# Replacing a scheduled work list by one that every engine follows literally, in an attention and mixer kernel on one core

## The chip, the cores and the metric

The kernel runs on one NeuronCore of a Trainium2 chip. The metric is the device time of one execution in microseconds; the number of record is the median of the timed runs. The core has five engines that are used here: TensorE (PE, with its weight loads shown as PEld), VectorE (DVE), ScalarE (ACT), GpSimd (POOL) and SyncE (SP), which only starts DMAs. Each engine works through its own queue of instructions in order and waits on semaphores.

## The reference

Inputs are q, k and v of shape (8 batches, 8 heads, 576 positions, 64), and four weight matrices. All are float32, and so is the output of shape (8, 576, 512).

```python
def _attn_ref(q, k, v):
    scores = scale * np.matmul(q, k.transpose(0, 1, 3, 2))
    rel = pos[:, None] - pos[None, :]
    mask_plain = (rel >= 0) & (rel < window)                                # 32; heads 0 to 3
    mask_dil = (rel >= 0) & (rel < window * dilation) & (rel % dilation == 0)  # 32*4; heads 4 to 7
    scores = np.where(masks, scores, -1e9)
    attn = softmax(scores)
    return attn @ v
def _moe_ref(x, w_tok1, w_tok2, w_ch1, w_ch2):       # x: (8, 576, 512), heads side by side
    xt = x.transpose(0, 2, 1)
    h = np.maximum(xt @ w_tok1, 0.0) @ w_tok2        # mixes positions, 576 -> 256 -> 576
    u = x + h.transpose(0, 2, 1)
    h2 = np.maximum(u @ w_ch1, 0.0) @ w_ch2          # mixes channels, 512 -> 1536 -> 512
    return u + h2
```

## The kernel before

The kernel handles the eight batches one after the other in a software pipeline: while PE does the channel mixing of batch n, the attention and the token mixing of batch a = n + 1 are worked in between.

**Loads.** `load_qk` brings q or k of four heads (a "kind": 0 for the plain window, 1 for the dilated one) into one buffer `lqk` with five DMAs; there are four such buffers, filled in the order q0, k0, q1, k1. `load_v` brings v with five larger DMAs into `lv`. All of these are started by SP, as are the copies inside the chip: `shift_v` (2 DMAs), `perm_v` (8 DMAs, rows of v in the dilated order), `x_perm` and `x_perm4` (4 DMAs each, attention results back to the natural order, for positions 0 to 511 and 512 to 575), and the output DMAs in `y_out`. The weights are loaded by POOL's queue in `wload`, which converts them to 16 bits on the way.

**Attention.** The loaded pieces are converted to 16 bits (`cast_qk`, `cast_v`; on POOL, for batch 0 on DVE), transposed on PE with the copy out on ACT (`tr`), and multiplied in small blocks (`qk_run`, three units u = 0, 1, 2, each with two halves). Each half goes through `sm_max` (DVE: mask add and row maximum), `sm_sub` (POOL: subtract), `sm_exp` (ACT), `sm_tr` (DVE: transposes of 32x32 blocks). `av_run` multiplies with v in three PSUM banks per kind and `av_out` (DVE) divides by the row sums.

**Mixing.** `h1_` and `u_` are the two matmuls of the token mixing; the last two matmuls of each `h1_` read the rows that `x_perm4` brings. `ut_` transposes the result. `m1_` (matmuls named gp, results gt) and `y_mm` (matmuls named yp) are the channel mixing, 12 blocks and 5 row tiles per batch; `y_out` adds u and starts the output DMA.

**Order.** Each of these steps is put in a list with `at(t, fn, ...)`, where t is a hand-written time, and the list is emitted sorted by t. In the kernel before, that order is only a priority: a planner in the compiler, which has its own cost model, picks for each engine the next instruction that it holds to be ready. So the order in each engine's queue can differ from the list. `gate` writes one element of `w1` from `lqk[("q", 1)]`, so that the load of `w1` comes after q1 has landed; nothing holds back the other weights.

Of the kernel before, what the change touches and what calls it, by code (L numbers as in the profile page):

```python
# [15 lines left out]
B = 8  # L16
H = 8
S = 576
# [4 lines left out]
NEG = -1.0e30  # L23

# [5 lines left out]
def _np_masks():  # L30
    q = np.arange(32)[:, None]
    j = np.arange(64)[None, :]
    base = np.where((j > q) & (j <= q + 32), 0.0, NEG).astype(np.float32)
    first = base.copy()
    first[:, 0:32] = NEG
    m8 = np.zeros((4, 32, 2, 2, 4, 64), dtype=np.float32)
    for g in range(4):
        for s in range(4):
            m8[g, :, 0, :, s] = (first if (s == 0 and g == 0) else base)[:, None]
            m8[g, :, 1, :, s] = (first if s == 0 else base)[:, None]  # L40
    m4 = np.broadcast_to(base[None], (4, 32, 64))
    return (np.ascontiguousarray(m8.reshape(128, 2, 8, 64)),
            np.ascontiguousarray(m4.reshape(128, 1, 64)))
# [3 lines left out]
def kernel(  # L47
# [15 lines left out]
    items = []  # L63

# [4 lines left out]
    m8_np, m4_np = _np_masks()  # L69
    ident = sb.tile([128, 128], FP16, tag="ident", name="ident")  # L70
    mask8 = sb.tile([128, 2, 8, 64], FP32, tag="mask8", name="mask8")
    mask4 = sb.tile([128, 1, 64], FP32, tag="mask4", name="mask4")
# [4 lines left out]
    qT = [one([128, 4, QTW], FP16, f"qT{i}") for i in range(2)]  # L77
    kT = [one([128, 4, KTW], FP16, f"kT{i}") for i in range(2)]
# [14 lines left out]
    def init():  # L93
        nc.scalar.dma_start(out=ident, in_=nc.inline_tensor(np.eye(128, dtype=np.float16), name="ident128").ap())
        nc.scalar.dma_start(out=mask8, in_=nc.inline_tensor(m8_np, name="mask8_d").ap())
        nc.scalar.dma_start(out=mask4, in_=nc.inline_tensor(m4_np, name="mask4_d").ap())
        for i in range(2):
            e = nc.vector
            e.memset(qT[i][:, :, S:QTW], 0.0)
            e.memset(kT[i][:, :, 0:KTO], 0.0)  # L100
            e.memset(kT[i][:, :, KTO + S:KTW], 0.0)
# [8 lines left out]
        nc.vector.memset(w1b[0:64], 0.0)  # L110

# [40 lines left out]
    def tr(n, nm, kind, hh, eng):  # L152
        src = cq[(nm, kind)]
        hp = 2 * kind + hh
        p = ps.tile([128, 1024], FP16, tag="tp", bufs=2, name=f"tp_{nm}_{n}_{hp}")
# [6 lines left out]
        dst, o = (qT[n % 2], 0) if nm == "q" else (kT[n % 2], KTO)  # L162
# [8 lines left out]
    def qk_mm(n, sc, cell, kind, hh, s):  # L171
        par, hp = hh % 2, 2 * kind + hh // 2
        r0 = 64 * par
        for g in range(4):
            if kind == 0:
                t0 = 128 * s + 32 * g
                lhs = qT[n % 2][r0:r0 + 64, hp, t0:t0 + 32]
                rhs = kT[n % 2][r0:r0 + 64, hp, KTO + t0 - 32:KTO + t0 + 32]
            else:
                t0 = 128 * s + g  # L180
                lhs = qT[n % 2][r0:r0 + 64, hp, t0:t0 + 125:4]
                rhs = kT[n % 2][r0:r0 + 64, hp, KTO + t0 - 128:KTO + t0 + 125:4]
            yield dict(out=sc[32 * g:32 * g + 32, cell, :], lhsT=lhs, rhs=rhs, start=True, stop=True)
# [32 lines left out]
    def sm_max(n, u, par):  # L216
# [4 lines left out]
        if u < 2:  # L221
            nc.vector.tensor_tensor(out=s32, in0=sc, in1=mask8[:, u], op=ALU.add)  # L222
        else:
            a0, a1 = bass.broadcast_tensor_aps(sc[:, 0:4], mask4)
# [27 lines left out]
    BANKS = [(14, 20), (0, 7), (7, 14)]  # L252

    def av_run(n, kind):
        V_own = (vp if kind == 0 else vd)[n % 2]
        V_prv = (vs if kind == 0 else vd)[n % 2]
        for bi, (c0, c1) in enumerate(BANKS):
            av = ps.tile([128, 7, 65], FP32, tag="at", bufs=3, name=f"av_{n}_{kind}_{bi}")
            for c in range(c0, c1):
                s, hh = c // 4, c % 4  # L260
                par, kk = hh % 2, hh // 2
                if s < 4:
                    aT, cell = AT[(n, kind, par)], 4 * kk + s
                else:
                    aT, cell = AT[(n, 2, par)], 2 * kind + kk
                for half in (1, 0):
                    for g in range(4):
                        skip_prev = s == 0 and (kind == 1 or g == 0)
                        if half == 0 and skip_prev:
                            continue  # L270
                        rows = slice(32 * g, 32 * g + 32)
                        if half == 1:
                            rhs = V_own[rows, s, hh, :]
                        elif kind == 0:
                            rhs = V_prv[rows, s, hh, :]
                        else:
                            rhs = V_prv[rows, s - 1, hh, :]
                        nc.tensor.matmul(  # L278
                            out=av[rows, c - c0, :], lhsT=aT[rows, cell, half, :], rhs=rhs,
                            start=(half == 1), stop=(half == 0 or skip_prev),  # L280
                            tile_position=(32 * g, 32 * g),
                        )
            AV[(n, kind, bi)] = av
# [26 lines left out]
    H1, U, UT, GT, YP = {}, {}, {}, {}, {}  # L310
    MX = 3

    def mxp(name):
        return ps.tile([128, 512], FP32, tag="mx", bufs=MX, name=name)

    def h1_(n, jb):
# [9 lines left out]
        nc.tensor.matmul(out=p[:, 256:512], lhsT=w1b[:, js], rhs=x4, start=False, stop=True)  # L326
        t = sb.tile([128, DM], FP16, tag="h1", bufs=4, name=f"h1_{n}_{jb}")
# [3 lines left out]
    def u_(n, s):  # L331
        p = mxp(f"up_{n}_{s}")
        x = X[n]
        if s < 4:
            for jb in range(2):
                nc.tensor.matmul(out=p, lhsT=w2[:, jb, 128 * s:128 * s + 128], rhs=H1[(n, jb)],  # L336
                                 start=(jb == 0), stop=(jb == 1))
            t = sb.tile([128, DM], FP16, tag="u16", bufs=8, name=f"u16_{n}_{s}")
            nc.vector.tensor_tensor(  # L339
                out=t.rearrange("p (a c) -> p a c", a=2), in0=p.rearrange("p (a c) -> p a c", a=2),  # L340
                in1=x[:, :, 4 * s:4 * s + 4, :].rearrange("p a h d -> p a (h d)"), op=ALU.add)
        else:
            for jb in range(2):
                for a in range(2):
                    nc.tensor.matmul(out=p[64 * a:64 * a + 64, 0:256], lhsT=w2[:, jb, 512:576],
                                     rhs=H1[(n, jb)][:, 256 * a:256 * a + 256],
                                     start=(jb == 0), stop=(jb == 1))
            t = sb.tile([128, 256], FP16, tag="u16_4", bufs=2, name=f"u16_{n}_4")
# [4 lines left out]
    def ut_(n, s, eng):  # L353
# [4 lines left out]
        nb = 4 if s < 4 else 2  # L358
        for cb in range(nb):
            nc.tensor.transpose(out=p[:, 128 * cb:128 * cb + 128], in_=t[:, 128 * cb:128 * cb + 128],  # L360
                                identity=ident)
        if s < 4:
# [10 lines left out]
    def m1_(n, mb):  # L373
        t = sb.tile([128, S], FP16, tag="gt", bufs=14, name=f"gt_{n}_{mb}")
        for sh in range(2):
            p = mxp(f"gp_{n}_{mb}_{sh}")
            for cb in range(4):
                nc.tensor.matmul(out=p[:, 0:288], lhsT=w3[:, cb, 128 * mb:128 * mb + 128],  # L378
                                 rhs=UT[n][:, cb, 288 * sh:288 * sh + 288],
                                 start=(cb == 0), stop=(cb == 3))  # L380
            dst = t[:, 288 * sh:288 * sh + 288]
            if sh == 0 or mb % 3 == 2:
                nc.scalar.activation(out=dst, in_=p[:, 0:288], func=AF.Relu)  # L383
            else:
                nc.vector.tensor_scalar_max(out=dst, in0=p[:, 0:288], scalar1=0.0)  # L385
        GT[(n, mb)] = t

    def y_mm(n, s, m0, m1):
# [12 lines left out]
        if m1 == 12:  # L401
            y_out(n, s)
# [14 lines left out]
    def wload(i):  # L417
        g = nc.gpsimd
        if i == 0:
            g.dma_start(out=w1, in_=moe_w_tok1[0:512, :].rearrange("(s p) j -> p s j", p=128))  # L420
            g.dma_start(out=w1a[0:64], in_=moe_w_tok1[512:576, :])
            g.dma_start(out=w1b[64:128], in_=moe_w_tok1[512:576, :])
            g.dma_start(out=w2, in_=moe_w_tok2.rearrange("(j p) t -> p j t", p=128))
        elif i < 5:
            c = 384 * (i - 1)
            g.dma_start(out=w3[:, :, c:c + 384],
                        in_=moe_w_ch1[:, c:c + 384].rearrange("(c p) m -> p c m", p=128))
        else:
            m = 3 * (i - 5)
            g.dma_start(out=w4[:, m:m + 3],  # L430
                        in_=moe_w_ch2[128 * m:128 * m + 384, :].rearrange("(m p) c -> p m c", p=128))

    def gate(src):
        nc.gpsimd.tensor_copy(out=w1[0:1, 0, 0:1], in_=src)


    P = 36.0
    TM = 60.0

    def tm(n):  # L440
        return TM + n * P

    KEYS = [("q", 0), ("k", 0), ("q", 1), ("k", 1)]

    def softmax(n, u, t):
        at(t, qk_run, n, u)
        for par in range(2):
            o = 1.5 * par
            at(t + 0.6 + o, sm_max, n, u, par)
            at(t + 2.0 + o, sm_sub, n, u, par)  # L450
            at(t + 3.2 + o, sm_exp, n, u, par)
            at(t + 4.4 + o, sm_tr, n, u, par)

    def attention(n, tcast, ttr, dtr, tqk, tavd, tavp, engs, tload=None):
        for i, (nm, hq) in enumerate(KEYS):
            at(tcast + 1.4 * i, cast_qk, n, nm, hq, engs[i % len(engs)])
# [108 lines left out]
```

## Time and profile before

| | |
|---|---|
| Median of 3 runs | 416.58 us (413.0 to 416.91) |
| Profiled execution | 419.19 us, span 417.4 us |
| PE busy | 322.4 us (77%) |
| DVE, ACT, POOL busy | 205.6, 130.6, 103.9 us |
| Mean granted PE clock | 0.95 |
| First gp matmul of batch 0 | 73.0 us after the start |

Times inside the profile count from the start of the span. A row of a timeline gives start, length, engine, line and operation; rows of the same kind that follow each other are merged, with their count behind x. SPq is SP's queue at work on starting a DMA. In groups the numbers behind the bar are busy time in us, mean ns of one, and the idle time before, with what ended it.

### The profile page before, as it was taken

The numbers are of one execution on the slowest core, as the hardware profiler recorded it, in microseconds if no ns is written. First come the engines' busy times: TensorE is split into PE (matmuls) and PEld (weight loads), VectorE is DVE, ScalarE is ACT, GpSimd is POOL, SyncE is SP. The second block draws the span as 40 slices with busy tenths as digits, with TensorE's granted clock in tenths as the row PEclk, the third lists the DMA queues.
The fourth block names the chain that finished last, engine by engine and source line by source line (L and its number), as shares of the span: only waits on it lengthen the run. The fifth ranks groups of instructions, "written<-read, shape, count | busy, mean of one in ns | idle before, by whom it ended". The sixth has DMA issues, their size and how long they took to land.

```text
span 417.4 us, 12992 instructions
## 1 busy us (share of the span) xinstructions
PE 322.4 (77%) x5680; PEld 204.4 (49%) x5680; DVE 205.6 (49%) x435; ACT 130.6 (31%) x273; POOL 103.9 (25%) x107
## 2 busy tenths in 40 slices
PE   0113148999399969869489989878998899799995
PEld 0012033854158536545336655655565556564763
DVE  4015743383344944863416743873277518764322
ACT  1113102740038305440513515341445133521420
POOL 7001322273106503530611224322333001300000
PEclk9999997999599989998869999998999899999999
DMA  9999246967365866395765567661310111012102
GB/s 186 192 207 219 63 106 151 196 161 167 94 136 149 173 162 171 87 210 149 157 146 152 129 135 202 163 128 37 130 39 2 33 51 59 9 31 78 38 27 88
DMA packets 131240, 50.24 MB, mean 120 GB/s; under 512 B 117360, under 2 KB 123888, under 8 KB 131184
## 3 DMA queue, kind: packets, MB, share of 16 engines
q1 hardware_dynamic: 126080, 45.06, 46.3%
q0 software_dynamic: 4672, 3.77, 5.6%
q8 instruction: 44, 0.72, 0.8%
q10 hardware_dynamic: 432, 0.59, 0.4%
q14 instruction: 12, 0.10, 0.1%
HBM read 36.44 MB, written 9.44 MB: 110 GB/s over the span
## 4 chain that ended last, share of the span: by engine, by line
PE 52%; SPq 18%; DVE 13%; issue 6%; DMA 3%; POOL 3%; ACT 3%; POOLq 0%; DVEq 0%
PE yp L394 20%; PE gp L378 12%; SPq L118 11%; PE av L278 5%; DVE mx L226 3%; PE h1p L321 3%; POOL s L232 3%; PE up L336 3%; DVE s L222 3%; SPq L126 2%; PE tpu L360 2%; ACT e L237 2%; PE tp_k L157 2%; DMA lk<-in_k_dram 2%; PE tp_q L157 2%
## 5 line engine op out<-in xcount | busy, mean ns | idle before, releaser
L378 PE MATMUL gp<-uT,w 128*128 128x288 f16 x768 | 108.7, 291 | 13.9 <-ACT gt L383 7.6
L378 PEld LDWEIGHTS <-w 128*128 128x128 f16 x768 | 73.3, 99 | 40.4 <-issue 21.0
L394 PE MATMUL yp<-w,gt 128*128 128x512 f16 x384 | 91.4, 391 | 2.2 <-issue 1.9
L232 POOL TENSOR_TENSOR s<-s,mx 128x512 f32<-128x512 f32 (+1 forms) x48 | 42.8, 899 | 102.4 <-DVE mx L226 93.6
L383 ACT ACTIVATE gt<-gp 128x288 f16<-128x288 f32 x128 | 50.4, 408 | 46.1 <-PE gp L378 42.0
L394 PEld LDWEIGHTS <-gt 128*128 128x128 f16 x384 | 37.4, 100 | 46.1 <-issue 8.0
L408 DVE TENSOR_TENSOR o<-yp,u 128x512 f32<-128x512 f32 x32 | 22.0, 689 | 67.4 <-PE yp L394 65.7
L385 DVE TENSOR_SCALAR gt<-gp 128x288 f16<-128x288 f32 x64 | 28.5, 449 | 29.0 <-PE gp L378 28.4
L164 ACT COPY qT<-tp_q 128x576 f16<-128x576 f16 x32 | 19.3, 643 | 71.0 <-PE tp_q L157 71.0
L237 ACT ACTIVATE e<-s 128x512 f16<-128x512 f32 (+1 forms) x48 | 26.7, 559 | 45.0 <-POOL s L232 45.0
L278 PEld LDWEIGHTS <-aT 32*32 32x32 f16 x2400 | 24.9, 94 | 30.4 <-issue 19.4
L245 DVE STREAM_TRANSPOSE aT<-e 128x512 f16<-128x512 f16 (+1 forms) x48 | 29.5, 618 | 17.0 <-ACT e L237 16.9
L133 POOL CAST cq<-lq 128x1280 f16<-128x1280 f32 x14 | 17.5, 1252 | 74.2 <-PE tp_q L157 42.7
L321 PE MATMUL h1p<-x,w 128*128 128x512 f16 x64 | 21.6, 472 | 13.3 <-DMA x<-xd 13.3
L164 ACT COPY kT<-tp_k 128x576 f16<-128x576 f16 x32 | 19.9, 641 | 28.5 <-PE tp_k L157 28.5
L226 DVE TENSOR_REDUCE mx<-s 128x8 f32<-128x512 f32 (+1 forms) x48 | 27.5, 577 | 0.2
L157 PE MATMUL tp_q<-ident,cq 128*128 128x128 f16 x160 | 13.4, 230 | 17.8 <-DVE cq L133 17.6
L328 ACT ACTIVATE h<-h1p 128x512 f16<-128x512 f32 x16 | 9.4, 597 | 56.4 <-PE h1p L326 56.4
L157 PE MATMUL tp_k<-ident,ck 128*128 128x128 f16 x160 | 14.4, 230 | 14.9 <-DVE ck L133 14.3
L222 DVE TENSOR_TENSOR s<-sc,mask 128x512 f32<-128x512 f32 x32 | 21.0, 676 | 9.5 <-PE sc L190 9.3
L339 DVE TENSOR_TENSOR u<-up,x 128x512 f16<-128x512 f32 x32 | 21.0, 686 | 9.3 <-PE up L336 8.9
L278 PE MATMUL av<-vd,aT 32*32 32x65 f16 x1152 | 14.2, 197 | 13.9 <-DMA vd<-vn 11.1
(58 smaller groups left out, 300.1 us busy)
## 6 DMA issues: line engine op xcount, KB each, us to landing
lq<-in_q_dram SPq DMA_DIRECT2D x64, 128.0 KB, 3.8
lk<-in_k_dram SPq DMA_DIRECT2D x64, 128.0 KB, 3.4
lv<-in_v_dram SPq DMA_DIRECT2D x32, 256.0 KB, 4.0
out_dram<-o SPq DMA_DIRECT2D x32, 256.0 KB, 2.3
w<-in_moe_w_ch_dram POOLq DMA_DIRECT2D x8, 384.0 KB, 15.8
vd<-vn SPq DMA_DIRECT2D x32, 65.0 KB, 2.1
x<-xd SPq DMA_DIRECT2D x32, 64.0 KB, 2.1
vs<-vp SPq DMA_DIRECT2D x8, 243.8 KB, 2.9
```

The costliest lines, as they stand in the source:

```text
L118: nc.sync.dma_start(out=t[0:np_, s], in_=src[n, 4 * kind:4 * kind + 4, 128 * s:128 * s + np_, :].rearrange("h p d -> p h d"),)
L157: nc.tensor.transpose(out=p[:, 128 * s:128 * s + 128], in_=src[:, s, 2 * hh:2 * hh + 2].rearrange("p a d -> p (a d)"), identity=ident,)
L164: nc.scalar.copy(out=dst[:, hp, o:o + S], in_=p[:, 0:S])
L222: nc.vector.tensor_tensor(out=s32, in0=sc, in1=mask8[:, u], op=ALU.add)
L226: nc.vector.tensor_reduce(out=mx[:, 0:nc_, 0], in_=s32[:, 0:nc_], op=ALU.max, axis=AX.X)
L232: nc.gpsimd.tensor_tensor(out=s32[:, 0:nc_], in0=a0, in1=a1, op=ALU.subtract)
L237: nc.scalar.activation(out=e16[:, 0:nc_], in_=s32[:, 0:nc_], func=AF.Exp, scale=0.125)
L278: nc.tensor.matmul(out=av[rows, c - c0, :], lhsT=aT[rows, cell, half, :], rhs=rhs, start=(half == 1), stop=(half == 0 or skip_prev), tile_ ...
L321: nc.tensor.matmul(out=p, lhsT=w1[:, s, js], rhs=x[:, :, 4 * s:4 * s + 4, :].rearrange("p a h d -> p a (h d)"), start=(s == 0), stop=False)
L378: nc.tensor.matmul(out=p[:, 0:288], lhsT=w3[:, cb, 128 * mb:128 * mb + 128], rhs=UT[n][:, cb, 288 * sh:288 * sh + 288], start=(cb == 0), s ...
L383: nc.scalar.activation(out=dst, in_=p[:, 0:288], func=AF.Relu)
L394: nc.tensor.matmul(out=p, lhsT=GT[(n, mb)][:, 128 * s:128 * s + 128], rhs=w4[:, mb], start=(mb == 0), stop=(mb == 11))
```

## The change

Five things change together.

1. **Literal order.** The list is emitted inside `tc.manual_schedule()`. Every engine, SP and POOL included, then issues its instructions exactly in the order of the list.
2. **A new list.** Its times are no longer fixed offsets in a period of 36 us. `place` walks a hand-written row of PE pieces (tokens: m and y for channel mixing, h, u, x for token mixing and its transposes, T for the transposes of q and k, Q for the scores, D and A for the value products of the dilated and plain heads) and adds up durations from the table `DUR`; each piece's follow-up on another engine is placed a little behind it. `need` moves a piece behind the time at which its inputs are expected. Matmuls and their evacuation, which were one function, are now two entries (`m1_mm`/`m1_out`, and so on), as are `tr_mm`/`tr_out`.
3. **Value products bank by bank.** `av_run` handles one PSUM bank per call, and other matmuls stand between the banks.
4. **Weights held back.** Every weight DMA on POOL now has its own one-element `gate`: the token weights and the first quarter of `w3` wait for k1 of batch 0, the rest of `w3` waits for v of batch 0, `w4` waits for k1 of batch 1; and the first load of batch 1 waits for the last quarter of `w3`.
5. **Small things.** The transposed q and k (`qT`, `kT`) have one buffer instead of two. The mask of 512 KB is built on chip from one of 96 KB. The banks are counted from the front.

The core of the diff:

```diff
+    BANKS = [(0, 7), (7, 14), (14, 20)]
+    def av_run(n, kind, bi):
...
+    def wload_ch1(i, after):
+        c = 384 * i
+        gate(w3[0:1, 0, c:c + 1], after)
+        nc.gpsimd.dma_start(out=w3[:, :, c:c + 384], ...)
...
+        elif kind in "DA":
+            _, a, bi = tok
+            kd = int(kind == "D")
+            t = need(t, ("s", a, kd), ("s", a, 2), ("v", a, kd))
+            at(t, av_run, a, kd, bi)
+            at(t + d + LAT, av_out, a, kd, bi)
+            ready(("x", a), t + d + LAT + 0.9)
+            if bi == 2:
+                at(t + d + LAT + 1.2, x_perm if kd else x_perm4, a)
+                ready(("x", a), t + d + LAT + 1.2 + 2.2)
...
+    def casts(a, ts, eng, load=True):
+        for i in range(4):
+            at(ts[i], cast_qk, a, *KEYS[i], eng[i % len(eng)])
+            ready(("c", a, i), ts[i] + 1.3)
+            if load:
+                loads_after(ts[i] + 1.3, a, i)
+        at(ts[4], cast_v, a, 0, eng[-1])
+        at(ts[4] + 1.3, shift_v, a)
+        at(ts[5], cast_v, a, 1, eng[-1])
+        at(ts[5] + 1.3, perm_v, a)
...
+        if load:
+            loads_after(ts[5] + 1.4, a, 4)
...
+    casts(0, [4.0, 7.0, 10.0, 13.5, 20.0, 21.0], [nc.vector], load=False)
...
+    t = run(-1, 24.5, [("D", 0, 0), ("D", 0, 1), ("D", 0, 2), ("A", 0, 2), ("A", 0, 0), ("A", 0, 1)])
...
+        if n == 0:
+            at(28.0, lambda: nc.gpsimd.tensor_copy(out=lqk[("q", 0)][0:1, 0, 0, 0:1], in_=w3[0:1, 0, 384 * 3:384 * 3 + 1]))
+            for i in range(4):
+                at(28.1, load_qk, 1, *KEYS[i])
+            at(28.2, load_v, 1)
+            for i in range(4):
+                at(30.0 + 0.1 * i, wload_ch2, i, lqk[("k", 1)][0:1, 0, 0, 0:1])
...
+        else:
+            toks = (M(0, 1) + [("Q", a, 1)] + M(2, 3, 4) + [("Q", a, 2)] + M(5, 6, 7) + [("D", a, 0)] + M(8)
+                    + [("D", a, 1)] + M(9) + [("D", a, 2)] + M(10) + [("A", a, 2)] + M(11) + [("A", a, 0)]
+                    + Y(0, 0) + [("A", a, 1)] + Y(0, 1) + Y(1) + T(a + 1, 0, 1) + [("h", 0), ("h", 1)]
+                    + T(a + 1, 2, 3) + Y(2, 0) + [("u", 0), ("u", 1)] + Y(2, 1) + T(a + 1, 4)
+                    + [("u", 2), ("u", 3)] + Y(3, 0) + T(a + 1, 5) + [("x", 0), ("x", 1)] + Y(3, 1) + T(a + 1, 6)
+                    + [("x", 2), ("x", 3), ("u", 4)] + Y(4) + T(a + 1, 7) + [("x", 4), ("Q", a + 1, 0)])
+            if a + 1 < B:
+                casts(a + 1, [t + 3.0, t + 5.5, t + 8.0, t + 10.0, t + 12.5, t + 15.0], G)
...
+    if MANUAL:
+        with tc.manual_schedule():
+            for _, _, fn, a in todo:
+                fn(*a)
```

More of the change, by code (lines that the diff above doesn't have):

```diff
@@ L23 @@
 NEG = -1.0e30
+MANUAL = True
 QTW = 640
@@ L35, in _np_masks @@
     first[:, 0:32] = NEG
[L36 to L43, printed above, removed]
+    m = np.zeros((4, 32, 3, 64), dtype=np.float32)
+    m[:, :, 0] = base[None]
+    m[:, :, 1] = base[None]
+    m[0, :, 1] = first
+    m[:, :, 2] = first[None]
+    return np.ascontiguousarray(m.reshape(128, 3, 64))
 @with_exitstack
@@ L433, in gate @@
[L433 to L452, printed above, removed]
@@ new lines, with later @@
+    M = lambda *ks: [("m", k_) for k_ in ks]
+    Y = lambda s, h=None: [("y", s, 0, 12)] if h is None else [("y", s, 6 * h, 6 * h + 6)]
+    T = lambda a, *is_: [("T", a, i) for i in is_]
+    G = [nc.gpsimd]
+    def later(n, toks):
+        return [x for x in toks if not (x[0] in "TQDA" and x[1] >= B) and not (n + 1 >= B and x[0] in "hux")]
+    at(-100, init)
+    for nm, kd in KEYS:
+        at(-99, load_qk, 0, nm, kd)
+    at(-99, load_v, 0)
+    at(13.0, wload_tok, lqk[("k", 1)][0:1, 0, 0, 0:1])
```

386 lines of the change are left out of this document (220 added, 166 removed).

## The prediction

> **What bounds the kernel now.** I read the page's chain of waits first, then the timelines of PE and SP, batch by batch.
>
> ```profile
> PE 52%; SPq 18%; DVE 13%; issue 6%; DMA 3%; POOL 3%; ACT 3%; POOLq 0%; DVEq 0%
> ```
>
> Only half of the chain is PE's, and the second name is SP's queue. The first gp matmul of each batch cuts the span into a prologue and eight periods (PE's timeline; the first two rows and the last are from the chain of waits):
>
> ```profile
> 73.00 1.05 PE gp L378 x8
> 122.47 3.01 PE gp L378 x24
> ...
> 168.74 2.13 PE L378 MATMUL gp<-uT,w 128*128 128x288 f16 x16
> 225.74 0.54 PE L378 MATMUL gp<-uT,w 128*128 128x288 f16 x3
> 264.90 1.15 PE L378 MATMUL gp<-uT,w 128*128 128x288 f16 x8
> 309.12 1.15 PE L378 MATMUL gp<-uT,w 128*128 128x288 f16 x8
> 352.46 1.15 PE L378 MATMUL gp<-uT,w 128*128 128x288 f16 x8
> ...
> 389.50 11.87 PE gp L378 x96
> ```
>
> Prologue 73.0; periods of n = 0 to 7: 49.5, 46.3, 57.0, 39.2, 44.2, 43.3, 37.0, 27.9 (the last to 417.4). The best full period is 39.2; the 57.0 of n = 2 is the one to understand. There SP worked without a pause through one round of its work:
>
> ```profile
> 178.50 3.12 SPq L118 DMA_DIRECT2D lq<-in_q_dram  x5
> 181.72 2.85 SPq L118 DMA_DIRECT2D lk<-in_k_dram  x5
> 184.67 3.96 SPq L118 DMA_DIRECT2D lq<-in_q_dram  x5
> 188.72 4.01 SPq L118 DMA_DIRECT2D lk<-in_k_dram  x5
> 192.84 0.59 SPq L141 DMA_DIRECT2D vs<-vp  x1
> 193.47 0.59 SPq L142 DMA_DIRECT2D vs<-vp  x1
> 194.16 3.17 SPq L147 DMA_DIRECT2D vd<-vn  x4
> 197.38 2.49 SPq L149 DMA_DIRECT2D vd<-vn  x4
> 199.91 5.55 SPq L126 DMA_DIRECT2D lv<-in_v_dram  x5
> ...
> 206.17 2.44 SPq L302 DMA_DIRECT2D x<-xd  x4
> 208.65 2.48 SPq L307 DMA_DIRECT2D x<-xd  x4
> ```
>
> About 0.6 us per DMA, over 1 us for v, and 32.6 us from the first load (178.50) to the end of `x_perm4` (211.13). PE waited for just that:
>
> ```profile
> 210.22 1.87 PE L321 MATMUL h1p<-x,w 128*128 128x512 f16 x4 [5.87 <-DMA x<-xd]
> 212.78 1.91 PE L321 MATMUL h1p<-x,w 128*128 128x512 f16 x4
> 214.91 3.06 PE L394 MATMUL yp<-w,gt 128*128 128x512 f16 x12
> ```
>
> In the other periods the planner started the q and k loads while PE was in the second half of the batch, so the round was over when h1 came. So the question for the change is where its list puts SP's round.
>
> **The steady periods, n = 2, 3, 4.** I added up the list's times. After a batch's first gp (call it M0), SP's entries stand in this order: the four q/k loads of batch a+2 (list times +4.3, +6.8, +9.3, +11.3), `shift_v` +13.8, `x_perm` +15.4, `perm_v` +16.3, `load_v` +16.4, `x_perm4` +17.0, then outputs. PE's h, which needs `x_perm4`, stands at +23.8. The list treats a DMA as free to issue; in a literal queue `x_perm4` stands behind 39 DMAs of the same round, none of them its input.
>
> The round cannot start earlier either: each load waits for the POOL cast that frees its buffer, the cast of q0 stands behind POOL's first `sm_sub`, and that waits for the score matmuls, PE's last piece before M0.
>
> ```profile
> L222 DVE TENSOR_TENSOR s<-sc,mask 128x512 f32<-128x512 f32 x32 | 21.0, 676 | 9.5 <-PE sc L190 9.3
> L226 DVE TENSOR_REDUCE mx<-s 128x8 f32<-128x512 f32 x32 | 21.3, 674 | 0.1
> L232 POOL TENSOR_TENSOR s<-s,mx 128x512 f32<-128x512 f32 x32 | 33.1, 1042 | 83.6 <-DVE mx L226 80.3 <-DMA lq<-in_q_dram 3.3
> L133 POOL CAST cq<-lq 128x1280 f16<-128x1280 f32 x14 | 17.5, 1252 | 74.2 <-PE tp_q L157 42.7 <-DMA lq<-in_q_dram 17.0 <-DMA vd<-vn 14.2
> ```
>
> Start of the round: 0.68 + 0.67 + 1.04 + 1.25 = 3.6, with 0.5 for semaphores (estimate) +4.1. The four loads take 4 x 2.85 = 11.4 at best and 14.2 by the stretch above; POOL's casts between its subs pace them too (k1's cast, behind six subs and three casts, ends near +13.6). I take their end at +17.8. Behind them: shift 1.2, `x_perm` 2.45, `perm_v` 5.0 to 5.7, v 4.3 to 5.6, `x_perm4` 2.5. The lower end for `perm_v` is twice the row of 2.49, that for v from a quieter stretch:
>
> ```profile
> 273.80 4.32 SPq L126 DMA_DIRECT2D lv<-in_v_dram  x5
> ```
>
> SP pauses in the new round, so I take the lower ends: 15.4, issue done at +33.2, and landing after 2.1:
>
> ```profile
> x<-xd SPq DMA_DIRECT2D x32, 64.0 KB, 2.1
> ```
>
> h ends its wait at +35.3 (bounds 34.0 and 38.0). PE without the wait is there at about +26.5: the list's +23.8 and 2.7 late. Of these, 1.7 are the waits for gt that gp had in each period already (13.9 over eight):
>
> ```profile
> L378 PE MATMUL gp<-uT,w 128*128 128x288 f16 x768 | 108.7, 291 | 13.9 <-ACT gt L383 7.6 <-issue 2.9 <-DVE gt L385 2.8
> ```
>
> The other 1.0 is an estimate for DVE, whose maxima, transposes and divisions now all stand in the gp stretch. So PE idles some 8 us. What follows h is as before:
>
> ```profile
> 294.55 1.03 PE L321 MATMUL h1p<-x,w 128*128 128x512 f16 x4
> 297.27 2.75 PE L394 MATMUL yp<-w,gt 128*128 128x512 f16 x12
> ```
>
> From 294.55 to the next M0 at 309.12 are 14.6; four matmuls (0.87) run ahead of the wait, so 13.7 remain. After the idle time PE is slow: in n = 2, after 5.87 idle, three groups took 1.87, 1.91 and 3.06 against 1.03, 1.03 and 2.75, which is 2.0, and with the small matmuls between them 2.5. Period 35.3 + 13.7 + 2.5 = 51.5, with bounds 47.7 (34.0, no slow stretch) and 54.7 (38.0 and 3.0). Against 57.0 + 39.2 + 44.2 = 140.4 stand 154.5: **+14.1** (bounds +2.7 and +23.7).
>
> The Trainium skill (TensorE: Matmul & The Clock Gate, part 1) says that an idle window of about 3.4 us halves the clock and about 3.4 us of sustained work restores it. By that the loss would be 1.7 instead of 2.5, and three periods 2.4 shorter; the three rows of n = 2 speak for more, and I keep 2.5.
>
> **n = 5, 6, 7.** n = 5 has no loads left, but `perm_v` still stands ahead of `x_perm4`: `x_perm` starts when DVE has divided the third dilated bank, about +18.9 (list +14.2, some 4 late behind DVE's transposes, 0.8 for itself; estimates); with 2.45 + 5.0 + 2.5 + 2.1 it lands at +30.9; 13.7 more is 44.6: **+1.3**. n = 6 has neither; its PE pieces are those of before: 37.0, **0** (bounds -1 and +1.5). n = 7 is pure channel mixing, 27.9, 0.
>
> **n = 0 and 1.** By the list h is at +28.9 in n = 0 and 10.0 remain. The third dilated bank is divided at +24, `x_perm` 2.45, one output 0.55, `x_perm4` 2.5, landing 2.1: +31.6, with DVE late by 1, +32.6. Period 32.6 - 0.9 + 10.0 = 41.7 against 49.5: **-7.8** (bounds -10 and -5). The gain is again SP's: before, `x_perm4` was out at 112.6, 39.6 after M0:
>
> ```profile
> 110.15 2.48 SPq L307 DMA_DIRECT2D x<-xd  x4
> ```
>
> In n = 1 the q/k loads stand after the last softmax unit (+15, with DVE late +16.4): loads 11.4 to 14.2, two outputs 1.1, both x copies 4.9, landing 2.1: +37; 10.2 remain after h; with 0.5 slow: 46.8, **+0.5** (bounds -2 and +3).
>
> **The prologue.** Before, the weights went out at once and stretched the first loads:
>
> ```profile
> 3.69 9.07 SPq L118 DMA_DIRECT2D lk<-in_k_dram  x5
> ```
>
> Held back, q and k take about 14 and v 5.5: v lands near 22. But POOL now waits for v in `wload_ch1` ahead of the subs of units 1 and 2, so they run from 25 to 28.3; DVE's second v cast stands behind two transposes that need them and ends near 30.5; `perm_v` issues until 35.5 and lands 37.6; the dilated banks are done at 39.3, `x_perm` issues until 41.8. Then the 25 loads of batch 1 stand ahead of `x_perm4`: 14 + 5 is 60.8, `x_perm4` until 63.3, landed at 65.4. Before, from h1 to the first gp:
>
> ```profile
> 62.78 3.57 PE h1p L321 x8
> ```
>
> 73.0 - 62.78 = 10.2, less 1.8 for four matmuls done early: first gp at 73.8, **+0.8** (bounds 69 and 78). What is saved on the first loads is spent in SP's order.
>
> **Edits without a price of their own.** Thirteen gates on POOL are one-element copies in waits that exist anyway. Single `qT`/`kT`: the list writes them only after the last score matmuls of the batch before, so no wait; else ACT's copies would shift by one unit. The smaller mask frees 0.4 MB at the start, where loads run unhindered. Value products bank by bank spread PE's smallest instructions; what they save ends ahead of h, where SP's round is later anyway. Without that cover it is worth at most the 19.4 us for which PE's weight loads in this line waited for nothing visible, 2.4 per batch:
>
> ```profile
> L278 PEld LDWEIGHTS <-aT 32*32 32x32 f16 x2400 | 24.9, 94 | 30.4 <-issue 19.4 <-DVE aT L245 8.4 <-PE av L278 0.8
> ```
>
> **Sum.** +0.8 - 7.8 + 0.5 + 14.1 + 1.3 = +8.9. On the span 417.4: 426.3; on the profiled execution 419.2: 428.1; that execution lies 2.6 above the median of the runs, so for the median **425**.
>
> **Rivals.**
> *PE-bound (faster).* If SP's round does not hold h up, every full period is PE's. The price is the best period of before, 39.2, for n = 0 to 5: 73.8 + 6 x 39.2 + 37.0 + 27.9 = 374. It decides if `x_perm4` lands by +26.5, a round of 20 us instead of 29; for it, that most periods before had no wait at h; against, the rows of 0.6 us per DMA and the list order. Chance 0.16.
> *The front gains (about equal).* Up to the second batch everything falls at its low end: v lands at 19, and batch 1's loads go out in 4 x 2.85 + 4.3 = 15.7. The first gp comes at 67.5, the first two periods are 39.5 and 44.3, and with the other terms the span is 415.3, the median 414.5. For it, nothing else loads then; against, the four rows from 178.50 took 3.5 on average. Chance 0.14.
> *DVE's queue (much slower).* Literal order lets each late exp hold DVE's queue, and gt copies queued behind it hold PE. Before, gp waited 13.9 us in all; 3 more per period for seven periods give 446. Chance 0.10.
> *Forecast.* 425, own range 408 to 442, chance 0.60.
>
> About 1% (4 us) is what a measurement of this kernel can tell from no change. Slower than 420.8: 0.47 of the forecast's 0.60, and 0.10 of DVE's: 0.57. Faster than 412.4: 0.16, 0.06 of the front's and 0.03 of the forecast's low end: 0.25. The rest, 0.18, is within. The range 402 to 446 leaves out the PE-bound case and a tail above.
>
> **What would show it.** In the profile after: periods near 51 in n = 2 to 4 and PE idle some 8 us inside the first h group, ended by the DMA x<-xd; SP's queue with `load_v` between `perm_v` and `x_perm4`; the first gp between 69 and 78, with h1 waiting for the 64-row copies. I am wrong if h1's wait there is under 2 us, if SP's DMAs go out faster than 0.5 us each, or if DVE is what PE waits for.

## The result and the profile after

The change made the kernel slower: 445.72 us, where 425 was forecast.

| | before | after |
|---|---|---|
| Median | 415.46 us of 4 runs (413.0 to 416.91) | 445.72 us of 4 runs (443.37 to 446.78) |
| Ratio of the times, 95% interval | | 1.073 (1.065 to 1.080) |
| Profiled execution, its span | 419.19, 417.4 us | 443.37, 441.6 us |
| PE busy | 322.4 us | 321.0 us |

PE does the same work in about the same time. The span grew by 24.2 us, and PE's idle time (span less busy) by 25.6, from 95.0 to 120.6. The summary of the chain of waits (page, part 4) after:

```profile
PE 49%; SPq 25%; DVE 9%; DMA 6%; issue 5%; POOL 3%; ACT 3%; POOLq 0%; DVEq 0%
```

SP's queue has risen from 18% to 25% of the chain, DVE has gone down from 13% to 9%. The group that heads PE's waits and the gp group (part 5: busy us, mean ns, then idle us before it and what ended most of that):

```profile
L393 PE MATMUL gp<-uT,w 128*128 128x288 f16 x768 | 105.7, 286 | 6.5 <-DVE gt L406 3.9
...
L330 PE MATMUL h1p<-x,w1a 128*128 128x256 f16 x16 | 5.8, 365 | 57.4 <-DMA x<-xd 57.4
```

57.4 us of PE's idle time now stand before one line, the first matmul of h1 that reads the rows copied by `x_perm4`. From the list of PE's waits before (us in total, times, longest), all of h1:

```profile
PE h1p L321 <- DMA x<-xd: 13.3, 3, 5.9
```

The places after, from PE's timeline (the number in brackets is the idle time before the row); the gp rows are the first gp matmuls of batches 2 to 6:

```profile
71.65 0.37 PE L330 MATMUL h1p<-x,w1a 128*128 128x256 f16 x1 [25.53 <-DMA x<-xd]
...
160.45 1.86 PE L326 MATMUL h1p<-x,w 128*128 128x512 f16 x4 [3.83 <-DMA x<-xd]
...
174.42 0.79 PE L393 MATMUL gp<-uT,w 128*128 128x288 f16 x5
...
210.87 0.37 PE L330 MATMUL h1p<-x,w1a 128*128 128x256 f16 x1 [10.81 <-DMA x<-xd]
...
227.23 1.03 PE L393 MATMUL gp<-uT,w 128*128 128x288 f16 x7
...
263.18 0.37 PE L330 MATMUL h1p<-x,w1a 128*128 128x256 f16 x1 [9.82 <-DMA x<-xd]
...
280.68 0.54 PE L393 MATMUL gp<-uT,w 128*128 128x288 f16 x3
...
316.69 0.37 PE L330 MATMUL h1p<-x,w1a 128*128 128x256 f16 x1 [8.18 <-DMA x<-xd]
...
333.05 0.79 PE L393 MATMUL gp<-uT,w 128*128 128x288 f16 x5
...
361.71 0.37 PE L330 MATMUL h1p<-x,w1a 128*128 128x256 f16 x1 [2.71 <-DMA x<-xd]
...
377.76 0.42 PE L393 MATMUL gp<-uT,w 128*128 128x288 f16 x2
```

The stretches from one batch's first gp to the next, as in the prediction, in us:

| | prologue | n=0 | 1 | 2 | 3 | 4 | 5 | 6 | 7 | span |
|---|---|---|---|---|---|---|---|---|---|---|
| before | 73.0 | 49.5 | 46.3 | 57.0 | 39.2 | 44.2 | 43.3 | 37.0 | 27.9 | 417.4 |
| predicted | 73.8 | 41.7 | 46.8 | 51.5 | 51.5 | 51.5 | 44.6 | 37.0 | 27.9 | 426.3 |
| after | 79.5 | 42.5 | 52.4 | 52.8 | 53.5 | 52.4 | 44.7 | 35.6 | 28.2 | 441.6 |

And SP's round in n = 2, of which the prediction showed that of before (timeline of SP's queue):

```profile
178.46 3.28 SPq L120 DMA_DIRECT2D lq<-in_q_dram  x5
...
188.86 3.79 SPq L120 DMA_DIRECT2D lk<-in_k_dram  x5
...
194.09 3.28 SPq L309 DMA_DIRECT2D x<-xd  x4
197.47 2.45 SPq L149 DMA_DIRECT2D vd<-vn  x4
199.96 2.49 SPq L151 DMA_DIRECT2D vd<-vn  x4
202.49 4.08 SPq L128 DMA_DIRECT2D lv<-in_v_dram  x5
206.67 2.47 SPq L314 DMA_DIRECT2D x<-xd  x4
```

The round begins 4.0 after the first gp (174.42). `perm_v` and `load_v` stand ahead of `x_perm4`, whose last DMA is out at 209.14, 34.7 after that gp, and the copies are there 1.7 later. This is the mechanism that was forecast, and every period from n = 2 to n = 4 has it. Where the new time came from, in span: prologue 6.5, n = 1 6.1, n = 2 to 4 18.3, n = 5 1.4, against 7.0 given back in n = 0 and 1.1 in n = 6 and 7.

### The profile page after: what moved, and what is told of

It is laid out like the page before. It is cut to its first block, busy times and chain, and to the rows that moved or that the text cites. A ratio compares the mean times of both kernels' runs of the same rounds, so it can differ in the third digit from the quotient of the medians.

```text
span 441.6 us, 13041 instructions
## 1 busy us (share of the span) xinstructions
PE 321.0 (73%) x5680; PEld 203.6 (46%) x5680; DVE 209.9 (48%) x440; ACT 132.3 (30%) x273; POOL 104.4 (24%) x119
## 4 chain that ended last, share of the span: by engine, by line
PE 49%; SPq 25%; DVE 9%; DMA 6%; issue 5%; POOL 3%; ACT 3%; POOLq 0%; DVEq 0%
PE yp L414 15%; PE gp L393 13%; SPq L120 9%; SPq L128 5%; PE av L285 3%; DMA x<-xd 3%; PE up L344 3%; PE h1p L326 3%; SPq L309 3%; SPq L314 3%; SPq L149 3%; DVE aT L252 2%; PE yp L418 2%; SPq L151 2%; PE tp_k L158 2%
## 5 line engine op out<-in xcount | busy, mean ns | idle before, releaser
L393 PE MATMUL gp<-uT,w 128*128 128x288 f16 x768 | 105.7, 286 | 6.5 <-DVE gt L406 3.9
L414 PE MATMUL yp<-w,gt 128*128 128x512 f16 x384 | 93.0, 389 | 0.1
L393 PEld LDWEIGHTS <-w 128*128 128x128 f16 x768 | 71.1, 98 | 28.8 <-issue 10.1
L404 ACT ACTIVATE gt<-gp 128x288 f16<-128x288 f32 x128 | 51.6, 410 | 41.1 <-PE gp L393 37.3
L330 PE MATMUL h1p<-x,w1a 128*128 128x256 f16 x16 | 5.8, 365 | 57.4 <-DMA x<-xd 57.4
L426 DVE TENSOR_TENSOR o<-yp,u 128x512 f32<-128x512 f32 x32 | 22.1, 691 | 50.5 <-PE yp L414 46.8
L285 PEld LDWEIGHTS <-aT 32*32 32x32 f16 x2400 | 24.1, 94 | 34.5 <-issue 28.5
L330 PEld LDWEIGHTS <-w1a 128*128 128x128 f16 x16 | 1.9, 119 | 63.4 <-issue 32.9
L233 DVE TENSOR_REDUCE mx<-s 128x8 f32<-128x512 f32 (+1 forms) x48 | 28.7, 597 | 1.7
L326 PE MATMUL h1p<-x,w 128*128 128x512 f16 x64 | 23.6, 503 | 4.4 <-DMA x<-xd 3.8
L285 PE MATMUL av<-vd,aT 32*32 32x65 f16 x1152 | 15.1, 196 | 15.7 <-DMA vd<-vn 11.2
L302 DVE RECIPROCAL rec<-av 128x7 f32<-128x7 f32 (+1 forms) x48 | 9.4, 196 | 27.2 <-PE av L285 26.5
```

The costliest lines, as they stand in the source:

```text
L233: nc.vector.tensor_reduce(out=mx[:, 0:nc_, 0], in_=s32[:, 0:nc_], op=ALU.max, axis=AX.X)
L285: nc.tensor.matmul(out=av[rows, c - c0, :], lhsT=aT[rows, cell, half, :], rhs=rhs, start=(half == 1), stop=(half == 0 or skip_prev), tile_ ...
L326: nc.tensor.matmul(out=p, lhsT=w1[:, s, js], rhs=x[:, :, 4 * s:4 * s + 4, :].rearrange("p a h d -> p a (h d)"), start=(s == 0), stop=False)
L414: nc.tensor.matmul(out=p, lhsT=GT[(n, mb)][:, 128 * s:128 * s + 128], rhs=w4[:, mb], start=(mb == 0), stop=(mb == 11))
```

## The experiments

The theory: it is the place of `x_perm4` in the literal queue of SP, behind DMAs that PE needs later. Rival A: the DMA engines are full, and the order on SP only decides which transfer is late. Rival B: the literal order of PE, DVE and ACT costs the time, and PE's wait for SP would be replaced by another. Times below are medians; the kernel before, on the same chips, had 417.4 (beside e1, e2, e4 and e5), 416.95 (e7 to e10) and 416.19 (e11 to e15). A kernel with one run has no interval; all runs but one of the kernel before lie between 413.0 and 419.7, so a difference of a few us between single runs says nothing by itself. Periods are taken from PE's timeline as above.

### Moving one place in the list

**e1_front**: the loads of batch 1 go behind `x_perm4` of batch 0.

```diff
-                at(28.1, load_qk, 1, *KEYS[i])
-            at(28.2, load_v, 1)
+                at(28.8, load_qk, 1, *KEYS[i])
+            at(28.9, load_v, 1)
```

> Only batch 0: the 25 loads of batch 1 stand behind x_perm4 in SP's order instead of ahead of it. Theory (place in SP's queue): x_perm4 goes out right behind x_perm near 45 us, h1's wait of 25.5 us for it falls to under 4, and the first gp comes at 56 to 60 instead of 79.5; part of that is lost again in the first period, since w4 and POOL's casts still wait for k1 of batch 1, so the whole is 15 to 23 us shorter, about 424. Rival A (DMA traffic, not order): the copies land as late as before, under 5 us gained. Rival B (literal order of the compute engines costs the time): under 5 us gained.

Measured: 438.4 (1 run), where some 424 were expected. The step did what it should in the prologue: first gp at 54.5 instead of 79.5, with no wait before h1. But n = 0 took 63.0 instead of 42.5, so of 25 us only 5 were left in the span of 436.6. PE's timeline:

```profile
63.82 1.25 PE L158 MATMUL tp_q<-ident,cq 128*128 128x128 f16 x10 [7.12 <-POOL cq L135]
...
89.06 0.27 PE L285 MATMUL av<-vd,aT 32*32 32x65 f16 x2 [4.06 <-DMA vd<-vn]
```

The first row waits for q of batch 1, which was now loaded later; the second for `perm_v` of batch 1, which SP issued from 86.2 on, behind 20 loads of batch 2. The wait moved to what was next in the same queue.

**e2_steady**: `perm_v` and `load_v` 1.0 later in the list from batch 3 on, so that `x_perm4` comes ahead of both.

```diff
-        at(ts[5] + 1.3, perm_v, a)
+        at(ts[5] + 1.3 + late, perm_v, a)
-            loads_after(ts[5] + 1.4, a, 4)
+            loads_after(ts[5] + 1.4 + late, a, 4)
-                casts(a + 1, [t + 3.0, ...], G)
+                casts(a + 1, [t + 3.0, ...], G, late=1.0)
```

> Only batches 3 to 7: perm_v and load_v stand behind x_perm4 in SP's order (both 1.0 later in the list), everything else as it was. Theory: the waits of h for x_perm4 (10.8, 9.8, 8.2, 2.7 us) fall under 1 us each and PE is not slowed after them, the periods of n = 2 to 4 go from 52.4 to 53.5 down to 41 to 43, n = 5 from 44.7 to about 41: 30 to 37 us in all, about 410. Rival A (DMA traffic): loads and copies share the same DMA engines, the wait moves to other DMAs, under 10 us gained. Rival B (literal order of the compute engines): nothing gained.

Measured: 433.0 (1 run), where some 410 were expected. h1's waits in n = 2 to 5 are gone (at most 1.0 in n = 2), n = 5 fell to 40.1, but n = 2 to 4 took 50.1, 50.1 and 50.9. The waits of PE and DVE in that kernel (us in total, times, longest):

```profile
PE yp L414 <- DVE o L426: 21.6, 3, 7.3
```

```profile
DVE o L426 <- DMA out_dram<-o: 24.0, 3, 8.1
```

The outputs now stand behind `perm_v` and `load_v`, both `o32` buffers are taken until they are out, DVE waits with the third sum, and PE with DVE: three times 7.3 at most, instead of three times 8 to 11.

**e5_all**: both, and in n = 1 the q and k loads of batch 4 behind `x_perm4` as well.

```diff
-            casts(3, [t + 14.0, ...], G)
+            casts(3, [t + 14.0, ...], G,
+                  lts=[t + 28.2 + 0.1 * i for i in range(4)])
```

> x_perm4 ahead of the loads everywhere: the edits of both experiments above, and in n = 1 the q and k loads of batch 4 behind x_perm4. Theory: gains add, 15 to 23 from the front, 30 to 37 from n = 2 to 5 and 8 to 10 from n = 1: 375 to 395, faster than both kernels, ratio to the kernel before 0.90 to 0.95. Rival A (DMA traffic): 420 or more. Rival B: 435 or more.

Measured: 430.0 (4 runs), ratio 1.033 (1.024 to 1.042). Expected were 375 to 395. Prologue 54.3 and n = 1 46.4 came down as they should, n = 0 went to 59.9, and n = 2 to 61.1, since the loads put off in n = 1 made its round late. The number alone would also fit rival A (420 or more); e7_early and e10_o6 below tell the two apart.

**e15_n1**: the third part alone (the edit just shown, nothing else).

> Only n = 1: the q and k loads of batch 4 stand behind x_perm4 in SP's order. Theory: h there no longer waits, the period of n = 1 falls from 52.4 to 43 to 45, of which some 2 us are the slow stretch of PE behind the wait; the loads now end in the next period, so n = 2 gets longer by 0 to 8. Rival (the compute engines are late by themselves in n = 1): 50 or more.

Measured: 451.3 (1 run). n = 1 45.3 instead of 52.4, so the loads ahead of `x_perm4` are what makes n = 1 long; but n = 2 64.5 instead of 52.8. PE's timeline in n = 2:

```profile
204.46 1.87 PE L326 MATMUL h1p<-x,w 128*128 128x512 f16 x4 [11.20 <-DMA x<-xd]
...
216.40 0.37 PE L330 MATMUL h1p<-x,w1a 128*128 128x256 f16 x1 [10.07 <-DMA x<-xd]
```

The 20 loads cost the next period 11.7, where 0 to 8 were expected, for the 7.1 they gave to this one. Three moves and their sum, each time the same answer: the theory is right about the place, and wrong if it is taken to mean that the place alone costs the time. An item put behind is late for its own reader.

### Who is held to the order

**e4_sched**: the same list, no engine held to it (`MANUAL = False`: the planner orders the queues, as in the kernel before).

> The new list as a priority only, with the planner choosing the order of every engine as in the kernel before. In the instruction lists SP's order of the steady batches is nearly the literal one (load_v still ahead of x_perm4). Theory: so the time stays within 10 us of the changed kernel, 435 to 455, with h waiting 8 us or more for x_perm4 in n = 2 to 4. Rival B (literal order of the compute engines costs the time): it falls to 425 or less.

Measured: 398.0 (1 run), span 395.9. **e8_pda** and **e9_sppool**: a part of the engines is held to it.

```diff
-        with tc.manual_schedule():
+        with tc.manual_schedule(engines={mybir.EngineType.PE, mybir.EngineType.DVE, mybir.EngineType.Activation}):   # e8_pda
+        with tc.manual_schedule(engines={mybir.EngineType.SP, mybir.EngineType.Pool}):   # e9_sppool
```

> PE, DVE and ACT follow the list literally; SP and POOL are left to the planner. The all-planner run gave 398 against 443 for the literal one, so the order in some queue costs 45 us. Theory (SP's round, and POOL's casts that start it): with these two queues free the time falls to 395 to 415. Rival B (literal order of the compute engines): it stays at 430 or more.

> The complement: only SP and POOL follow the list literally, the planner orders PE, DVE and ACT. Theory: the time stays at 425 to 450. Rival B: it falls to 400 to 410.

Measured: 406.5 and 424.5 (1 run each). The four spans together, in us:

| | SP, POOL by the planner | SP, POOL literal |
|---|---|---|
| PE, DVE, ACT by the planner | 395.9 (e4_sched) | 422.7 (e9_sppool) |
| PE, DVE, ACT literal | 404.7 (e8_pda) | 441.6 (after) |

So literal order costs 45.7 in all: 27 to 37 of them on SP and POOL, 9 to 19 on the compute engines, according to which is freed first (three of the four kernels have one run). The new list itself, with everything else in the change, is no loss: without literal order it is below the kernel before.

I had expected 435 to 455 from e4_sched, because SP's order in its instruction lists was nearly the literal one. SP's timeline in n = 3, whose first gp is at 213.97, shows what that leaves out:

```profile
203.25 1.70 SPq L120 DMA_DIRECT2D lq<-in_q_dram  x3
...
206.77 2.88 SPq L120 DMA_DIRECT2D lk<-in_k_dram  x5
...
229.06 1.21 SPq L128 DMA_DIRECT2D lv<-in_v_dram  x2
230.37 3.17 SPq L309 DMA_DIRECT2D x<-xd  x4
233.58 2.16 SPq L128 DMA_DIRECT2D lv<-in_v_dram  x3
235.84 2.47 SPq L314 DMA_DIRECT2D x<-xd  x4
```

These are the same round as in n = 3 of the kernel after. `load_v` does stand ahead of `x_perm4`, and with its pauses the round takes 35.1 us, more than the 30.4 there; but it starts 10.7 ahead of the first gp instead of 4.0 behind it. So `x_perm4` is out at +24.3 instead of +34.4, and h1 waits 1.1 for it instead of 9.8. Of the full periods only n = 2 still has a long wait, of 6.1. With the order nearly kept, it is when the round starts that decides.

Rival B has a part, and the smaller one. That part is not DVE's wait for late exps holding gt back, as the rival in the prediction had it: gp's idle time fell from 13.9 to 6.5. In n = 3 of e9_sppool `x_perm4` is as late as in the kernel after (+34.5), but h1 waits 5.7 instead of 9.8: between its first h1 group and the wait PE has the second group, twelve yp matmuls, the transposes and the scores, which in the kernel after stand behind the wait. So some of the part lies in PE's order; how much DVE and ACT add was not separated.

### Starting the round earlier, or cutting the chain behind it

**e7_early**: literal order, but from n = 2 on the POOL casts of q and k, and with them the loads they release, stand in the second half of the batch before, right behind PE's transposes of the old q and k. The core of the edit:

```diff
-                casts(a + 1, [t + 3.0, t + 5.5, t + 8.0, t + 10.0, t + 12.5, t + 15.0], G)
+                cast_v_all(a + 1, [None] * 4 + [t + 2.9, t + 4.2], G)
+                if a + 2 < B:
+                    casts_qk(a + 2, [t + 24.1, t + 26.7, t + 33.2, t + 37.8], G)
```

> Literal order on all engines, SP's order left as it is relative to x_perm4, but the round starts earlier: from n = 2 on, the q and k casts (and with them the loads that they free) stand right behind the transposes that free their buffers, in the second half of the batch before, and the v casts near its start. Theory: x_perm4 then has nothing long ahead of it when its data are ready; periods of n = 2 to 4 fall from 52.4 to 53.5 to 40 to 43, n = 5 from 44.7 to about 41, together 400 to 415. Rival A (DMA engines full): above 425. Rival B: 435 or more.

Measured: 413.8 (10 runs), ratio 0.993 (0.989 to 0.997), so within 1% of the kernel before. n = 3 to 5 took 40.1, 41.3 and 39.8; n = 2, the transition, still 50.5, where 40 to 43 were expected.

**e10_o6**: e2_steady with six `o32` buffers instead of two.

```diff
-            o = sb.tile([128, DM], FP32, tag="o32", bufs=2, ...)
+            o = sb.tile([128, DM], FP32, tag="o32", bufs=6, ...)
```

> As the run with perm_v and load_v behind x_perm4, but with six output buffers instead of two. There h no longer waited, yet the time was 433: PE's y matmuls waited 21.6 us for DVE's y_out, and that 24 us for output DMAs, which now stood behind perm_v and load_v in SP's queue. Theory (the same round, another last item): with enough buffers nobody waits for the output DMAs, and the time is 402 to 415. Rival A (the DMA engines themselves are full): the wait moves on again and the time stays above 425.

Measured: 410.2 (1 run). DVE waits for no output any more, and n = 2 to 5 took 41.9, 40.6, 41.8 and 39.9. What is left of PE's wait is the prologue's (25.8 of 29.8):

```profile
PE h1p L330 <- DMA x<-xd: 29.8, 5, 25.8
```

Two different edits take 10.6 to 13.4 us from each full period that they reach, one by starting SP's round ahead of its time, one by letting what stands behind `x_perm4` be late without harm. Both keep all DMAs and their sizes. Rival A is out for the steady periods: in n = 3 the DMA engines carry 107 GB/s in the kernel after, 142 in e10_o6 and 143 in e7_early, which is 5.7 to 5.8 MB each time, in 53.5, 40.6 and 40.1 us.

### The prologue

**e11_w4late**: the four loads of `w4` on POOL wait for v of batch 1 instead of k1.

```diff
-                at(30.0 + 0.1 * i, wload_ch2, i, lqk[("k", 1)][0:1, 0, 0, 0:1])
+                at(30.0 + 0.1 * i, wload_ch2, i, lv[0:1, 0, 0, 0:1])
```

> Only the gate of w4 is changed: it waits for v of batch 1 instead of k1 of batch 1, so that w4 is not on its way while SP starts load_v and x_perm4 for the first h1. Theory (the prologue term was short because w4 shares the DMA engines): load_v takes 5 to 6 us instead of 8.3, x_perm4 2.5 instead of 4.4 and lands 2 to 3 later instead of 5, the first gp comes at 73 to 75 instead of 79.5. Rival (SP's order alone set it, the copies are slow anyway): first gp at 78 or later. The whole may not follow, since w4 and POOL's casts of batch 1 come later.

Measured: 444.9 (1 run): first gp at 75.6 instead of 79.5; 73 to 75 were expected, and 78 or later from the rival. The chain of waits of the kernel after, through that stretch (start, length, what), and then SP's timeline of e11_w4late:

```profile
54.32 0.60 SPq L128
54.97 0.59 SPq L128
55.60 1.02 SPq L128
56.67 3.28 SPq L128
59.99 2.58 SPq L128
...
62.67 2.53 SPq L314
65.25 0.59 SPq L314
65.88 0.59 SPq L314
...
66.53 4.99 DMA x<-xd
...
79.54 0.49 PE gp L393 x4
```

```profile
54.21 4.78 SPq L128 DMA_DIRECT2D lv<-in_v_dram  x5
59.09 2.55 SPq L314 DMA_DIRECT2D x<-xd  x4
```

In the kernel after, POOL released the first piece of `w4` at 54.7; from 56.7 on three DMAs of SP in a row take 2.5 to 3.3 us each to start, where in n = 2 the same DMAs take 0.8 and 0.6 on average (4.08 for five, 2.47 for four). With `w4` held until 58.7 the five loads of v and the four copies take 7.3 instead of 12.7 us. The copies' landing was no faster (h1 starts at 66.93, 5.3 after the last issue): `w4` was then under way beside it. In e1_front, where `x_perm4` goes out from 41.9 to 45.1, ahead of `w4` and of the loads, h1 begins at 46.81 without a wait, so landing takes under 1.8 there. So the first 80 us are the one place where other traffic is seen to lengthen SP's work, as rival A has it. In e11_w4late the saving was lost again in the periods after (n = 0 44.5, n = 4 54.8).

**e13_front2**: literal order with e10_o6 and e1_front, the gates of `w4` behind three of POOL's casts of batch 1, and `perm_v` of batch 1 ahead of two of batch 2's loads.

```diff
+    (the edits of e1_front, e2_steady and e10_o6)
-                at(30.0 + 0.1 * i, wload_ch2, ...)
+                at(41.6 + 0.1 * i, wload_ch2, ...)
-            casts(1, [t - 1.0, ...], G)
+            casts(1, [t - 1.0, ...], G,
+                  lts=[t + 0.3, t + 2.5, t + 15.62, t + 15.62])
```

> Literal order. On top of the run with six output buffers: x_perm4 of batch 0 ahead of the loads of batch 1; w4's gates behind three of POOL's casts; and in n = 0 the shift and perm of v of batch 1 ahead of two of the four loads of batch 2, where the front edit alone lost its gain. Theory (places in SP's and POOL's queues): the first gp stays at 54 to 56 and the period of n = 0 is 46 to 50 instead of 63, so the gain of the front reaches the end: 384 to 395. Rival A (DMA engines full in the first 100 us): 402 or more.

Measured: 401.6 (4 runs), ratio 0.965 (0.958 to 0.971), slower than the 384 to 395 expected and just under the 402 that rival A was to give. First gp at 54.2, n = 2 to 4 41.8, 42.6 and 41.9, but n = 0 still 63.0, where 46 to 50 were expected: SP's timeline there, with `w4` again beside it:

```profile
57.89 9.87 SPq L128 DMA_DIRECT2D lv<-in_v_dram  x5
67.87 7.31 SPq L120 DMA_DIRECT2D lq<-in_q_dram  x5
```

Ten DMAs that take 7 to 8 us elsewhere (4.08 and 3.28 in n = 2 of the kernel after) took 17, so that the value products of batch 1 and then h came late (5.67 and 8.25 us of wait). No order that I tried gets the loads of batches 1 and 2 and `w4` through in time; where the prologue is short, n = 0 is long.

**e14_front2s**: the same list, no engine held to it.

> The list of the run above as a priority only, with the planner ordering all engines. Theory: with SP's and POOL's places mended in the list, the planner has little left to give: within 8 us of the literal run, 380 to 398. Rival B (literal order of the compute engines costs much by itself): 15 us or more below the literal run.

Measured: **386.2** (4 runs), ratio 0.927 (0.921 to 0.932), 7% faster than the kernel before, and the best version of the study. Here, with SP's order mended, literal order still costs 15.4 us (401.6 against 386.2), 6.7 of it in n = 0 (56.3 instead of 63.0). I had expected the two within 8 us of each other. In the planner's version gp waits more, 16.1 us instead of 5.9, but PE is idle less in all, 68.6 us instead of 80.5 (span less busy):

```profile
L393 PE MATMUL gp<-uT,w 128*128 128x288 f16 x768 | 108.2, 288 | 16.1 <-ACT gt L404 15.1
```

## Why the prediction was right, and where it was not

The forecast was 425, with an own range of 408 to 442; 445.72 lies above it. The direction and the mechanism in n = 2 to 4 were right, the size was not: the prologue and n = 1, where SP's queue was mis-priced, came out 11.3 longer than forecast between them. That the prediction's wider bounds, 402 to 446, just hold 445.72 is luck: 446 is the price of the rival on DVE's queue, which did not happen.

**Right: the place and the mechanism.** PE idles at the first h1 matmul that needs `x_perm4`, ended by the DMA x<-xd, in n = 2, 3 and 4 for 10.8, 9.8 and 8.2 (forecast: some 8), with `load_v` between `perm_v` and `x_perm4` on SP. e7_early and e10_o6 show it to be the cause: when this wait is taken away without making a new one, the periods are 40 to 42. One reading of the kernel before behind the forecast was wrong: its wait of 5.87 in n = 2 ended at 210.22, before `x_perm4` was out (211.13). It was for `x_perm`; the wait for `x_perm4` behind it was 0.31:

```profile
212.40 0.37 PE L325 MATMUL h1p<-x,w1a 128*128 128x256 f16 x1 [0.31 <-DMA x<-xd]
```

**n = 2 to 4: 154.5 forecast, 158.7 measured,** within the bounds. The round started at +4.0 (+4.1 forecast). h1 began at +36.4, +36.0 and +36.0 against +35.3; in n = 2 `x_perm` alone took 3.28 instead of 2.45. From h1 to the next gp it took 16.4, 17.5 and 16.4 against 16.2, but by two errors that nearly cancel. Without a long wait this stretch is 14.7 in the new list (e7_early n = 3 to 5, e10_o6 n = 2 to 5), not the 13.7 of before, so what follows h was not as before. And the slow stretch cost less: the granted clock was 0.50 until some 3.5 us after the wait in n = 2 and 4 and until some 5.8 after it in n = 3. Half of that is lost, by estimate 1.7 and 2.9, which with 14.7 gives 16.4 and 17.6. So of the two values that the prediction weighed, 1.7 was right in two periods of three, and the 2.5 that it kept was not.

**n = 0: 41.7 forecast, 42.5 measured; n = 6 and 7 together 64.9 and 63.8.** These terms hold.

**n = 5: 44.6 forecast, 44.7 measured, but by two errors that cancel.** h1 waited until +28.7, not +30.9 (`x_perm` could start 3 earlier than I put it), and what follows took 16.1, not 13.7: 1.0 is the longer stretch just named, and after a wait of 2.71 PE was slow there too, where I had given n = 5 no slow stretch. The timeline of PE behind that wait:

```profile
362.09 1.91 PE L326 MATMUL h1p<-x,w 128*128 128x512 f16 x4
...
366.24 1.03 PE L344 MATMUL up<-h,w 128*128 128x512 f16 x4
```

The first row is as long as after 5.87 us of idle time in the kernel before, and 4 us later a group of four is back at 1.03. The Trainium skill (TensorE: Matmul & The Clock Gate, part 1) says that an idle window of about 3.4 us halves the clock and about 3.4 us of sustained work restores it. The length of the slow stretch agrees: the granted clock was 0.50 from 361.2 to 364.5, and 1.00 from 364.6 on. The idle time does not: the wait began at 359.0, PE had been busy without a pause in the 4 us before, and the clock was 1.00 only until 361.1, so it fell after some 2.1 us of idle time. In e13_front2 a wait of 2.61, until 239.28, left it at 1.00. So a wait of this length may or may not cost the clock; what decides is not shown.

**Failed step 1, the prologue: 73.8 forecast, 79.5 measured (bound 78).** v and `x_perm` came when I said (`x_perm` issued from 39.0 to 42.3, forecast 39.3 to 41.8). The terms that were mis-sized are "14 + 5", "`x_perm4` until 63.3" and "landed at 65.4": `load_v` took 8.25 instead of 5, `x_perm4` 4.43 instead of 2.5, and landing 5.0 instead of 2.1. I took them from rows in which no weights load, though the change itself puts the release of `w4` (the wait for k1 of batch 1) just there. I had listed the gates as one-element copies with no price, and looked at what they make POOL wait for, not at what their DMAs meet. e11_w4late shows the two issue terms to come from the traffic of `w4`; for the landing it does not decide.

**Failed step 2, n = 1: 46.8 forecast, 52.4 measured (bound 49.8).** SP's timeline:

```profile
140.77 2.73 SPq L120 DMA_DIRECT2D lq<-in_q_dram  x5
...
147.19 4.17 SPq L120 DMA_DIRECT2D lq<-in_q_dram  x5
...
152.11 3.63 SPq L120 DMA_DIRECT2D lk<-in_k_dram  x5
156.16 2.68 SPq L309 DMA_DIRECT2D x<-xd  x4
158.94 2.43 SPq L314 DMA_DIRECT2D x<-xd  x4
```

The loads began 18.7 after the first gp, where I had put +16.4 (POOL's cast that frees the first buffer ended at 140.74), and with the two outputs between them ran to 155.74, 15.0 where the lower end of my sum was 12.5. `x_perm4` was out at +39.3, and h1's wait for it ended at +40.6, where I had put it at +37. What follows took 11.8, where my sum left 9.8: the slow stretch, which I had priced at 0.5, is a full one, as the row at 160.45 shows (1.86 for four matmuls). e15_n1 confirms the cause: without these loads ahead n = 1 is 45.3.

**The conversion.** The span came out 15.3 above the forecast, the median 20.7. The other 5.4 lie in the runs that were profiled: I took some 3 off for the median, as the profiled run of before lay above its own; that of after lay 2.4 below.

**The rivals.** PE-bound: not what happened, but its price was near. Where SP's round does not hold h1 up, full periods take 40 to 42 (39.2 forecast). The front gains: the opposite came, by the DMAs of `w4`. DVE's queue: gp's waits fell instead of rising. Outside all of them was that literal order would cost 45.7 us against the planner on the very same list. I compared the new order only with the old kernel, and so took two things for one: a list that, with the rest of the change, is some 20 us better (one run), and a rule of issuing that costs some 45.

## What to carry to other kernels

In a queue that issues in written order, add up the issue time of all that stands ahead of an item its reader is waiting for (here 39 DMAs, 28.2 us in n = 2), ask when the first of them can start, and do it for every item of the round: moving one item ahead of the others only pays if those put behind can be late, by an earlier start (e7_early) or by more buffers (e10_o6). A change that mixes a new order of work with a new rule of issuing should be tried with each alone: here the same list took 398.0 without the rule (one run) and 445.7 with it, and the list mended at SP's places 386.2 and 401.6. Take the time of a transfer from a row with the same neighbours that it will have.

## What the runs showed of the hardware

I had not expected that SP's time to start a DMA depends so much on what POOL has under way. The same five loads of v took 4.08 (n = 2), 4.78 (e11_w4late), 8.25 (after) and 9.87 us (e13_front2), the last two with the 384 KB pieces of `w4` beside them; a single start took up to 3.28 in the kernel after and 4.78 in e13_front2. So a busy issuing queue is not a fixed number of DMAs per us. From 56.7 to 66.5 in the kernel after, the DMA engines moved 200 GB/s at a busy share of 1.20 by the profile, in the loads of n = 2 (178.4 to 193.0) 159 GB/s at 0.71. That SP stands still because these engines are full is not shown, though: in e11_w4late, from 59.0 to 61.7, the share was 1.22, and the four copies were started in 2.55 us all the same.
